# An attention and MLP kernel: eight token tiles in the first group of the second product, and conversions moved behind the split of x

## The chip, the cores and the metric

The program runs on one core of one Trainium2 chip. A core has five engines that follow their own queues in order and meet through semaphores: TensorE (PE; its weight loads are listed apart as PEld), VectorE (DVE), ScalarE (ACT), GpSimd (POOL) and SyncE (SP), which here only starts transfers. The metric is the device time of one execution in microseconds; less is better. Before the change three runs took 959.28, 961.35 and 961.48 us, the median 961.35 us.

## The reference

Attention over 4 batches, 12 heads, 448 positions and head size 64, in which the scores are mixed over the heads before the softmax and after it, and then an MLP over the 1792 x 768 result:

```python
scores = scale * np.matmul(q, k.transpose(0, 1, 3, 2))
scores = np.einsum('bhij,hg->bgij', scores, w_pre)
attn = np.exp(scores - np.max(scores, axis=-1, keepdims=True))
attn = attn / (np.sum(attn, axis=-1, keepdims=True) + 1e-09)
attn = np.einsum('bhij,hg->bgij', attn, w_post)
x = np.matmul(attn, v)          # as (4 * 448, 768)
h = x @ w_in                    # (768, 2048)
g = s * np.maximum(h, 0.0) ** 2 + b
out = g @ w_out                 # (2048, 768)
```

The change lies in the MLP alone. The two weight matrices come as 64-bit floats.

## The kernel before

**Stages.** Attention runs to about 490 us of the trace. The MLP follows in two rounds (`r` 0 and 1), each over half of the 2048 hidden columns: eight tiles `f` of 128. A round has a first product, `gemm1_part` (line 247), which fills a PSUM tile `ph` of 128 hidden columns by the 448 tokens of one batch `b`, and a second product, `gemm2` (line 291), which for each half `oh` of the 768 output columns and each of 14 token tiles `it` of 128 adds up 8 tiles f. Each product is made of three matmuls (high by low, low by high, high by high), so that one token tile of the second product takes 24 matmuls of 384 columns. Round 0 stores its sums to DRAM (`part`), round 1 loads them (`acc`), adds them and writes `out`.

**Weights.** A weight unit is a 128 x 384 piece. Units 0 to 15 of a round are w_in (two for each f), the next 16 are w_out: eight f for oh = 0, then eight for oh = 1. So units 24 to 31 are the weights of oh = 1 in round 0, units 40 to 47 the second half of w_in in round 1, and units 56 to 63 the weights of oh = 1 in round 1. Each is loaded raw (`raw`, two buffers, lines 132 and 139), and then `conversion` (line 145) makes two 32-bit parts of it: one ACT instruction `mk` (line 153) that reads raw, and seven DVE instructions (lines 154 to 177), of which the last writes the low part of `w` (line 177). Only then is the load of the raw after next started on SP (line 180), since a raw buffer comes free. `convert_to(n)` emits conversions up to unit n at that place in the program; on each engine they stand in the order in which they are emitted.

**PSUM.** There are eight banks. Six are handed out in turn by `bank` (line 237), to `ph` tiles and to the tiles of the second product alike. The other two make up one tile with the tag `sc`, which attention used for its scores; the MLP uses it only for the first two `ph` of round 0.

**The second product's groups.** For oh = 0 the first group holds six token tiles (one in each bank of the ring) and goes over f outside and over the six tiles inside, so that a weight of a late f is needed later; then each of the other tiles goes alone over all f. For oh = 1 each tile goes alone from the start, so all eight weights are needed within its first 24 matmuls. When a group is done its tiles are evicted in order: in round 0 by an ACT copy to `ob` (line 307, two buffers) and a store on ACT's queue (line 308); in round 1 by a DVE add into `acc` (line 311), a store on ACT's queue (line 312) and, on SP, the load of the `acc` tile six places further on (line 288), which takes over the buffer of the tile just stored. Six acc tiles are loaded beforehand. After each group the loop emits conversions of the weights of oh = 1:

```python
if oh == 0:
    convert_to(min(u0 + NU + 8 + 2 * (its[-1] - 4), u0 + 2 * NU))
```

With a first group that ends at tile 5 these are two conversions, and two more after each of the next three tiles.

**The start of round 1.** The order of (b, f) is (0, 0) to (0, 3), then (1, 0) to (1, 3), then the rest. The x of batch 1 is kept in the buffers of three g tiles (tile `xg`), which come free when round 0's last matmul is done. So x is split into high and low parts during the first three steps i: two ACT copies each (line 223) and two DVE subtractions (line 232), and after them in each step one conversion (line 913).

Of the kernel before, what the change touches and what calls it, by code (L numbers as in the profile page):

```python
# [9 lines left out]
F32 = mybir.dt.float32  # L10
# [11 lines left out]
def talking_heads_attention__then__act_relu2_kernel(  # L22
# [17 lines left out]
    P = 128  # L40
# [37 lines left out]
    NU = 16  # L78
# [16 lines left out]
    ps = ctx.enter_context(tc.tile_pool(name="ps", bufs=1, space=PSUM))  # L95
# [86 lines left out]
    def convert_step(upto):  # L182

        if done["run"] is None:
            if done["conv"] >= min(upto, len(units)):
                return False
            done["run"] = conversion(done["conv"])
        try:
            next(done["run"])
        except StopIteration:  # L190
            done["run"] = None
            done["conv"] += 1
        return True

    def convert_to(n):
        while convert_step(n):
            pass
# [4 lines left out]
    NT = B * S // P  # L202
# [4 lines left out]
    def load_x(r, b, kc):  # L207
        raw = rp.tile([P, S], F32, tag="xraw", name=f"xraw_{r}_{b}_{kc}", bufs=NKC)
        nc.sync.dma_start(raw, xd[b][kc])
        xraw_t[r, b, kc] = raw  # L210

    def split_x(r, b, kc):
        raw = xraw_t.pop((r, b, kc))
        if b == 1:

            if kc % 2 == 0:
                x_u["g"] = mp.tile(
                    [P, 2, PT], F32R, tag=f"g{kc // 2}_1", name=f"xg_{r}_{kc}", bufs=1
                )
            x = x_u["g"][:, :, kc % 2 * S:kc % 2 * S + S]  # L220
        else:
            x = rp.tile([P, 2, S], F32R, tag="x", name=f"x_{r}_{b}_{kc}", bufs=NKC)
        nc.scalar.activation(x[:, 0, :], raw, AF.Copy)  # L223
        later.append((x[:, 1, :], raw, x[:, 0, :]))
        x_u[r, b, kc] = x
# [3 lines left out]
    def low_parts():  # L229
        while later:  # L230
            o, x, hi = later.pop(0)
            nc.vector.tensor_tensor(out=o, in0=x, in1=hi.bitcast(F32), op=ALU.subtract)  # L232

    banks = ["pm", "po", "pm", "po", "xp", "px"]
    turn = {"bank": 0}

    def bank(name):
        tag = banks[turn["bank"] % len(banks)]
        turn["bank"] += 1
        return ps.tile([P, 512], F32, tag=tag, name=name, bufs=banks.count(tag))  # L240

    def gemm1_part(r, b, f, kc, ph):
        w = w_u["in", r, f, kc // NKH]
        x = x_u[r, b, kc]
        c0 = kc % NKH * P
        for m, (i, y) in enumerate(((0, 1), (1, 0), (0, 0))):
            nc.tensor.matmul(  # L247
                ph[:, :S], w[:, i, c0:c0 + P], x[:, y, :],
                start=(kc == 0 and m == 0), stop=(kc == NKC - 1 and m == 2),
            )  # L250

    def relu2(r, b, f, ph):

        h = mp.tile([P, S], F32, tag="h", name=f"h_{r}_{b}_{f}", bufs=2)
        nc.scalar.activation(h, ph[:, :S], AF.Relu)  # L255
        nc.scalar.activation(h, h, AF.Square)
        nc.scalar.activation(h, h, AF.Identity, scale=sb[:, 0:1], bias=sb[:, 1:2])
        if b % 2 == 0:
            g_t[f, b // 2] = mp.tile(
                [P, 2, PT], F32R, tag=f"g{f}_{b // 2}", name=f"g_{r}_{f}_{b // 2}", bufs=1  # L260
            )
        g = g_t[f, b // 2]
        c0 = b % 2 * S
        nc.scalar.activation(g[:, 0, c0:c0 + S], h, AF.Copy)  # L264
        nc.gpsimd.tensor_tensor(  # L265
            out=g[:, 1, c0:c0 + S], in0=h, in1=g[:, 0, c0:c0 + S].bitcast(F32), op=ALU.subtract
        )
# [18 lines left out]
    def load_acc(oh, it):  # L286
        t = rp.tile([P, S], F32, tag="xraw", name=f"acc_{oh}_{it}", bufs=NKC)[:, :NO]
        nc.sync.dma_start(t, part[oh][it])
        acc_t[oh, it] = t

    def gemm2(r, oh, its):

        pos = [bank(f"po2_{r}_{oh}_{it}") for it in its]
        for f in range(NF):
            w = w_u["out", r, f, oh]
            for po, it in zip(pos, its):
                g = g_t[f, it * P // PT]
                c0 = it % (PT // P) * P
                for m, (x, y) in enumerate(((0, 1), (0, 0), (1, 0))):
                    nc.tensor.matmul(  # L300
                        po[:, :NO], g[:, x, c0:c0 + P], w[:, y, :],
                        start=(f == 0 and m == 0), stop=(f == NF - 1 and m == 2),
                    )
        for po, it in zip(pos, its):
            if r + 1 < NR:
                ob = mp.tile([P, NO], F32, tag="ob", name=f"ob_{oh}_{it}", bufs=2)
                nc.scalar.activation(ob, po[:, :NO], AF.Copy)
                nc.scalar.dma_start(part[oh][it], ob)
                continue
            ob = acc_t.pop((oh, it))  # L310
            nc.vector.tensor_tensor(out=ob, in0=po[:, :NO], in1=ob, op=ALU.add)
            nc.scalar.dma_start(out[it * P:(it + 1) * P, oh * NO:(oh + 1) * NO], ob)
            n = oh * NT + it + NKC
            if n < NOH * NT:
                load_acc(n // NT, n % NT)
# [348 lines left out]
    for ci in range(2, NCH):  # L664
        b, _, _ = chunks[ci]
# [51 lines left out]
    for s in range(NB + 4):  # L717
        spent = max(spent, -0.4) + load.get(s, 0)
        left, held = [], set()
        for x in fill:  # L720
            _, lo, hi, cost, order, f, args = x
# [145 lines left out]
    for r in range(NR):  # L867
        u0 = 2 * r * NU
        n = NHEAD if r == 0 else NF // 2
        order = [(b, f) for b in range(2) for f in range(n)]  # L870
        order += [(b, f) for f in range(n, NF) for b in range(2)]
        order += [(b, f) for b in range(2, B) for f in range(NF)]
        last = {b: i for i, (b, f) in enumerate(order)}
        wait = []

        takes = {0: (r, 2), 2: (r, 3)}
        if r + 1 < NR:
            takes[3] = (r + 1, 0)
        for i, (b, f) in enumerate(order):
            for b0, nxt in takes.items():  # L880
                if i == max(last[b0] - 7, 6):
                    for kc in range(NKC):
                        load_x(*nxt, kc)
            nxt = takes.get(b)
            if r > 0 and i == 0:
                for kc in range(NKC):
                    load_x(r, 1, kc)
            if (r, b) == (0, 0) and f < NHEAD:
                ph = head_t[f]
            else:  # L890
                ph = bank(f"ph_{r}_{b}_{f}")
                for kc in range(NKC):
                    gemm1_part(r, b, f, kc, ph)
                    if nxt and i == last[b] and b < B - 1:
                        split_x(*nxt, kc)
                        low_parts()
            wait.append((r, b, f, ph))

            if not any(i == last[b0] - 1 for b0 in (0, 2)):
                while wait:  # L900
                    relu2(*wait.pop(0))
            if nxt and i == last[b] and b == B - 1:
                for kc in range(NKC):
                    split_x(*nxt, kc)
                    low_parts()
            if r == 0 and b < 2:
                convert_to(min(2 * f + 8, NU))
            if r > 0 and i < 3:
                for kc in (2 * i, 2 * i + 1):
                    split_x(r, 1, kc)  # L910
                    low_parts()
            if r > 0:
                convert_to(u0 + min(i + 9, NU))
            if b == B - 1:
                convert_to(done["conv"] + 1)
        for oh in range(NOH):
            if r + 1 == NR and oh == 0:
                for it in range(NKC):
                    load_acc(0, it)
            if oh == 0:  # L920
                groups = [list(range(6))] + [[it] for it in range(6, NT)]
            else:
                groups = [[it] for it in range(NT)]
            for its in groups:
                gemm2(r, oh, its)
                if oh == 0:
                    convert_to(min(u0 + NU + 8 + 2 * (its[-1] - 4), u0 + 2 * NU))
                elif r + 1 < NR:
                    convert_to(min(u0 + 2 * NU + its[-1] + 1, u0 + 2 * NU + 8))
# [29 lines left out]
```

## Time and profile before

| | us |
|---|---|
| three runs | 959.28, 961.35, 961.48 |
| the profiled execution | 961.09 |
| its span in the trace | 959.4 |
| PE busy | 929.8 (97%) |
| PE weight loads busy | 786.2 (82%) |
| DVE busy | 639.0 (67%) |
| ACT busy | 597.7 (62%) |
| POOL busy | 398.1 (41%) |

The profiled execution took 1.69 us more than its span and lies 0.26 us under the median of the runs, so that a sum made in the trace can be set against the runs as it is. Busy is the union of an engine's instructions; for PE a busy engine is one whose matmuls follow each other, not one at its peak. In the rows a bracket behind an instruction gives the idle time of its engine just before it and what ended it. Shares of busy time say little here, since the MLP has stages with different limits; the rows further down are taken by stage.

### The profile page before, as it was taken

The numbers are of one execution on the slowest core, as the hardware profiler recorded it, in microseconds if no ns is written. First come the engines' busy times: TensorE is split into PE (matmuls) and PEld (weight loads), VectorE is DVE, ScalarE is ACT, GpSimd is POOL, SyncE is SP. The second block draws the span as 40 slices with busy tenths as digits, with TensorE's granted clock in tenths as the row PEclk, the third lists the DMA queues.
The fourth block names the chain that finished last, engine by engine and source line by source line (L and its number), as shares of the span: only waits on it lengthen the run. The fifth ranks groups of instructions, "written<-read, shape, count | busy, mean of one in ns | idle before, by whom it ended". The sixth has DMA issues, their size and how long they took to land.

```text
span 959.4 us, 19910 instructions
## 1 busy us (share of the span) xinstructions
PE 929.8 (97%) x7538; PEld 786.2 (82%) x7538; DVE 639.0 (67%) x1307; ACT 597.7 (62%) x1321; POOL 398.1 (41%) x469
## 2 busy tenths in 40 slices
PE   8899999999999999999999999999999999999998
PEld 4566767777777777777789999999998999999998
DVE  3899999888878888788678217656707711848311
ACT  5678778787888888877777977322216787711000
POOL 3866676666767667766613423100001332310000
PEclk9999999999999999999999999999999999999999
DMA  4665545654455544645323312245431410237431
GB/s 114 173 155 154 151 126 146 180 129 151 106 147 143 135 118 127 157 116 168 112 71 106 109 55 70 66 126 154 132 133 45 154 58 1 82 110 209 145 98 50
DMA packets 124252, 114.63 MB, mean 119 GB/s; under 512 B 61656, under 2 KB 120044, under 8 KB 124156
## 3 DMA queue, kind: packets, MB, share of 16 engines
q1 hardware_dynamic: 114630, 101.69, 38.3%
q10 hardware_dynamic: 9366, 11.59, 3.4%
q8 instruction: 59, 0.97, 0.4%
q14 instruction: 37, 0.30, 0.1%
q0 software_dynamic: 160, 0.09, 0.1%
HBM read 58.28 MB, written 16.52 MB: 78 GB/s over the span
## 4 chain that ended last, share of the span: by engine, by line
PE 64%; ACT 15%; DVE 13%; DMA 5%; issue 2%; POOL 0%; SPq 0%; ACTq 0%; DVEq 0%
PE po L300 24%; PE ph L247 17%; PE xp L517 6%; PE po L621 5%; ACT S L499 5%; PE sc L489 5%; PE pm L578 5%; ACT pm L585 4%; ACT eh L599 3%; DVE eh L606 3%; DVE A L637 2%; DVE st L580 2%; DMA raw<-in_moe_w_out_dram 2%; DMA nq<-in_q_dram 1%; PE trk L442 1%
## 5 line engine op out<-in xcount | busy, mean ns | idle before, releaser
L300 PE MATMUL po<-w,g 128*128 128x384 f32 x1344 | 234.6, 336 | 2.4 <-ACT h L255 2.4
L300 PEld LDWEIGHTS po<-w,g 128*128 128x128 f32 x1344 | 233.7, 188 | 3.1 <-ACT h L255 3.1
L564 POOL TENSOR_TENSOR hl<-blk,hl 120x448 fp32r<-120x448 f32 x180 | 206.0, 1145 | 15.0
L265 POOL TENSOR_TENSOR g<-h,g 128x448 fp32r<-128x448 f32 x64 | 77.9, 1217 | 287.9 <-ACT g L264 274.8
L621 PEld LDWEIGHTS <-eh 120*128 120x128 f16 (+1 forms) x2160 | 115.0, 98 | 63.4 <-DVE eh L606 40.5
L247 PE MATMUL ph<-x,w 128*128 128x448 f32 x810 | 166.2, 364 | 0.0
L247 PEld LDWEIGHTS ph<-x,w 128*128 128x128 f32 x810 | 152.0, 188 | 12.2
L563 POOL TENSOR_SCALAR hl<-blk 120x448 fp32r<-120x448 f32 x180 | 105.1, 584 | 136.2 <-PE pm L578 123.1
L621 PE MATMUL po<-wpost,eh 120*128 120x120 f16 (+1 forms) x2160 | 144.7, 217 | 14.6 <-DVE eh L606 14.1
L585 ACT ACTIVATE pm<-pm,st 120x448 f32<-120x448 f32 x180 | 109.8, 610 | 56.8 <-DVE st L580 56.2
L606 DVE SCALAR_TENSOR_TENSOR eh<-pm,st,eh 120x448 f16<-120x448 f32 x180 | 122.1, 679 | 16.6 <-ACT eh L599 13.2
L599 ACT ACTIVATE eh<-pm,st 120x448 f16<-120x448 f32 x180 | 114.1, 634 | 20.3 <-DVE st L597 17.2
L580 DVE TENSOR_REDUCE st<-pm 120x1 f32<-120x448 f32 x180 | 110.9, 616 | 22.0 <-PE pm L578 20.4
L637 DVE COPY A<-po 128x480 f32<-128x480 f32 x168 | 106.8, 635 | 0.0
L578 PE MATMUL pm<-hl,wpre_hi 120*120 120x448 f32 x360 | 101.9, 364 | 0.7 <-POOL hl L564 0.7
L153 ACT ACTIVATE mk<-raw 128x384 f32<-128x384 f32 x64 | 35.5, 554 | 93.7 <-DMA raw<-in_moe_w_out_dram 43.9
L517 PE MATMUL xp<-A,v 128*64 128x110 f32 (+1 forms) x1536 | 93.7, 265 | 0.0
L499 ACT ACTIVATE S<-sc 110x896 f32<-110x896 f32 (+1 forms) x91 | 83.3, 916 | 13.7 <-PE sc L489 11.5
L489 PE MATMUL sc<-Tk,Tq 64*110 64x448 f32 (+1 forms) x576 | 82.9, 393 | 2.3 <-ACT S L499 1.0
L578 PE MATMUL pm<-hl,wpre_lo 120*120 120x448 f32 x180 | 83.3, 463 | 0.1
L517 PEld LDWEIGHTS xp<-A,v 128*64 128x64 f32 x1536 | 74.2, 136 | 9.9 <-issue 1.2
L232 DVE TENSOR_TENSOR x<-xraw,x 128x448 fp32r<-128x448 f32 x36 | 23.9, 698 | 75.0 <-ACT x L223 75.0
(77 smaller groups left out, 1008.3 us busy)
## 6 DMA issues: line engine op xcount, KB each, us to landing
blk<-S SPq DMA_DIRECT2D x172, 210.0 KB
raw<-in_moe_w_in_dram SPq DMA_DIRECT2D x32, 384.0 KB
raw<-in_moe_w_out_dram SPq DMA_DIRECT2D x32, 384.0 KB
xraw<-xd SPq DMA_DIRECT2D x48, 224.0 KB
part<-ob ACTq DMA_DIRECT2D x28, 192.0 KB
acc<-part SPq DMA_DIRECT2D x28, 192.0 KB
out_dram<-acc ACTq DMA_DIRECT2D x28, 192.0 KB
v<-in_v_dram SPq DMA_DIRECT2D x24, 192.0 KB
```

The lines of the kernel that those rows point to most:

```text
L247: nc.tensor.matmul(ph[:, :S], w[:, i, c0:c0 + P], x[:, y, :], start=(kc == 0 and m == 0), stop=(kc == NKC - 1 and m == 2),)
L300: nc.tensor.matmul(po[:, :NO], g[:, x, c0:c0 + P], w[:, y, :], start=(f == 0 and m == 0), stop=(f == NF - 1 and m == 2),)
L489: nc.tensor.matmul(sc[e][:n, :S], qt[r0:r0 + D, p, x, :n], kt[r0:r0 + D, y, :], start=(m == 0), stop=(m == 2),)
L499: nc.scalar.activation(s_t[ci][:n, 2 * p:2 * p + 2, :], x_t["two"][:n, :, :S], AF.Copy, scale=SCALE)
L517: nc.tensor.matmul(xp[e * D:(e + 1) * D, p % 4, :n], vt[:, e, c, :], a[:, c, 2 * p + e, :n], start=(c == 0), stop=(c == NC - 1),)
L564: nc.gpsimd.tensor_tensor(out=hl[:n, 1, :], in0=blk[:n], in1=hl[:n, 0, :].bitcast(F32), op=ALU.subtract)
L578: nc.tensor.matmul(pm[:n, :S], w[:n, :n], hl[:n, x, :], start=(m == 0), stop=(m == 2))
L580: nc.vector.tensor_reduce(out=st[:n, 0:1], in_=pm[:n, :S], axis=AX.X, op=ALU.max, negate=True)
L585: nc.scalar.activation(e[:n], e[:n], AF.Exp, bias=st[:n, 0:1], accum_out=pm[:n, S:S + 1])
L599: nc.scalar.activation(eh[:n, 0, :], e[:n], AF.Copy, scale=st[:n, 3:4])
L606: nc.vector.scalar_tensor_tensor(out=eh[:n, 1, :], in0=e[:n], scalar=st[:n, 3:4], in1=eh[:n, 0, :], op0=ALU.mult, op1=ALU.subtract,)
L621: nc.tensor.matmul(po[:, c * BP:(c + 1) * BP], eh[:n, x, j0:j0 + P], wpost[:n, y].rearrange("p g i -> p (g i)"), start=(m == 0), stop=(m = ...
```

## The change

The first group of the second product for oh = 0 gets eight token tiles. The two more are put in the two banks of the `sc` tile, and they are the first two of the group; the six of the ring follow. Since the loop's formula is kept, the conversions emitted after that group are six instead of two. At the start of round 1 the conversions of steps 0 to 2 are left out there and come later: one for each step from step 3 on.

```diff
     def gemm2(r, oh, its):
 
-        pos = [bank(f"po2_{r}_{oh}_{it}") for it in its]
+        pos = []
+        if len(its) > len(banks):
+            two = ps.tile([P, 2, 512], F32, tag="sc", name=f"po2_{r}_{oh}")
+            pos = [two[:, 0], two[:, 1]]
+        pos += [bank(f"po2_{r}_{oh}_{it}") for it in its[len(pos):]]
         for f in range(NF):
...
-            if r > 0:
-                convert_to(u0 + min(i + 9, NU))
+            if r > 0 and i > 2:
+                convert_to(u0 + min(i + 6, NU))
...
             if oh == 0:
-                groups = [list(range(6))] + [[it] for it in range(6, NT)]
+                groups = [list(range(8))] + [[it] for it in range(8, NT)]
```

On ACT, behind the first group of round 0 (ob_0_5 is the eviction of tile 5, part its store, mk_24 the first ACT step of conversion 24), there stands before:

```order
L307 ACTIVATE ob_0_5_9577<-po2_0_0_5_9417 128x384
L308 DMA part0_5_71<-ob_0_5_9577 128x384
L153 ACTIVATE mk_24_9581<-raw_24_9354 128x384
L153 ACTIVATE mk_25_9594<-raw_25_9410 128x384
L307 ACTIVATE ob_0_6_9631<-po2_0_0_6_9606 128x384
L308 DMA part0_6_72<-ob_0_6_9631 128x384
L153 ACTIVATE mk_26_9635<-raw_26_9591 128x384
L153 ACTIVATE mk_27_9648<-raw_27_9604 128x384
```

On the same engine at the same place the changed program has (its lines from 294 on are four further down):

```order
L311 ACTIVATE ob_0_5_9626<-po2_0_0_5_9416 128x384
L312 DMA part0_5_71<-ob_0_5_9626 128x384
L311 ACTIVATE ob_0_6_9629<-po2_0_0_6_9417 128x384
L312 DMA part0_6_72<-ob_0_6_9629 128x384
L311 ACTIVATE ob_0_7_9632<-po2_0_0_7_9418 128x384
L312 DMA part0_7_73<-ob_0_7_9632 128x384
L153 ACTIVATE mk_24_9636<-raw_24_9354 128x384
L153 ACTIVATE mk_25_9649<-raw_25_9410 128x384
L153 ACTIVATE mk_26_9662<-raw_26_9646 128x384
L153 ACTIVATE mk_27_9675<-raw_27_9659 128x384
L153 ACTIVATE mk_28_9688<-raw_28_9672 128x384
L153 ACTIVATE mk_29_9701<-raw_29_9685 128x384
```

The evictions of tiles 6 and 7 moved ahead of mk_24, and six mk now stand in a row, with the eviction of tile 8 behind them.

On DVE, behind the first group of round 1 (acc_0_5 is the add of tile 5, u_56 the first DVE step of conversion 56), there stands before:

```order
L311 TENSOR_TENSOR acc_0_4_11523<-po2_1_0_4_11531,acc_0_4_11523 128x384
L311 TENSOR_TENSOR acc_0_5_11525<-po2_1_0_5_11532,acc_0_5_11525 128x384
L154 TENSOR_SCALAR u_56_11703<-raw_56_11475 128x384
L158 SCALAR_TENSOR_TENSOR u_56_11703<-raw_56_11475,u_56_11703 128x384
L162 TENSOR_SCALAR raw_56_11475<-raw_56_11475 128x384
```

On DVE the changed program has there:

```order
L315 TENSOR_TENSOR acc_0_4_11522<-po2_1_0_4_11529,acc_0_4_11522 128x384
L315 TENSOR_TENSOR acc_0_5_11524<-po2_1_0_5_11530,acc_0_5_11524 128x384
L315 TENSOR_TENSOR acc_0_6_11727<-po2_1_0_6_11531,acc_0_6_11727 128x384
L315 TENSOR_TENSOR acc_0_7_11731<-po2_1_0_7_11532,acc_0_7_11731 128x384
L154 TENSOR_SCALAR u_56_11759<-raw_56_11474 128x384
L158 SCALAR_TENSOR_TENSOR u_56_11759<-raw_56_11474,u_56_11759 128x384
```

The adds of tiles 6 and 7, whose acc tiles are not among the six loaded beforehand, moved ahead of conversion 56.

On DVE at the start of round 1 (xg is the split x of batch 1, u_40 the first step of conversion 40) there stands before:

```order
L232 TENSOR_TENSOR xg_1_0_10442<-xraw_1_1_1_10406,xg_1_0_10442 128x448
L154 TENSOR_SCALAR u_40_10449<-raw_40_10193 128x384
L158 SCALAR_TENSOR_TENSOR u_40_10449<-raw_40_10193,u_40_10449 128x384
L162 TENSOR_SCALAR raw_40_10193<-raw_40_10193 128x384
L167 SCALAR_TENSOR_TENSOR w_40_10447<-mk_40_10448,u_40_10449 128x384
L171 SCALAR_TENSOR_TENSOR raw_40_10193<-raw_40_10193 128x384
L175 TENSOR_SCALAR u_40_10449<-w_40_10447 128x384
L177 SCALAR_TENSOR_TENSOR w_40_10447<-raw_40_10193,u_40_10449 128x384
L232 TENSOR_TENSOR xg_1_2_10486<-xraw_1_1_2_10408,xg_1_2_10486 128x448
```

On DVE the changed program has there:

```order
L232 TENSOR_TENSOR xg_1_0_10441<-xraw_1_1_1_10405,xg_1_0_10441 128x448
L232 TENSOR_TENSOR xg_1_2_10472<-xraw_1_1_2_10407,xg_1_2_10472 128x448
L232 TENSOR_TENSOR xg_1_2_10472<-xraw_1_1_3_10409,xg_1_2_10472 128x448
L232 TENSOR_TENSOR xg_1_4_10503<-xraw_1_1_4_10411,xg_1_4_10503 128x448
L232 TENSOR_TENSOR xg_1_4_10503<-xraw_1_1_5_10413,xg_1_4_10503 128x448
L154 TENSOR_SCALAR u_40_10536<-raw_40_10192 128x384
```

All six subtractions stand together, and the conversions moved behind them.

## Rows read from the trace of the kernel before

**Rows 1.** Windows by stage: stretch, length, busy of each engine, granted clock, DMA.
```profile
605.00:718.00 113.00, 113.00 (x652) 113.00 (x651) 58.50 (x131) 26.28 (x53) 1.48 (x1) 1.00 0.40 126
```
**Rows 2.** Waits of PE in the MLP (490 to 960): us, times, longest.
```profile
PE po L300 <- ACT h L255: 2.4, 2, 1.2
PE ph L247 <- DVE xg L232: 1.6, 1, 1.6
```
**Rows 3.** Timeline of PE at its three waits: start us, us, instruction [idle before].
```profile
600.49 2.77 PE L300 MATMUL po<-w,g 128*128 128x384 f32 x15
604.46 7.75 PE L300 MATMUL po<-w,g 128*128 128x384 f32 x43 [1.20 <-ACT h L255]
...
737.44 4.73 PE L247 MATMUL ph<-xg,w 128*128 128x448 f32 x22 [1.55 <-DVE xg L232]
...
841.31 8.96 PE L300 MATMUL po<-w,g 128*128 128x384 f32 x50 [1.24 <-ACT h L255]
```
**Rows 4.** Chain of waits, 570 to 960: start us, us, what.
```profile
600.41 2.93 DMA raw<-in_moe_w_out_dram
...
604.46 114.52 PE po L300 x657
...
828.80 4.97 DMA raw<-in_moe_w_out_dram
...
841.31 114.54 PE po L300 x657
```
**Rows 5.** Timeline of ACT behind the first group of round 0.
```profile
624.55 0.49 ACT L307 ACTIVATE ob<-po 128x384 f32<-128x384 f32 x1 [14.87 <-PE po L300]
...
627.04 0.49 ACT L307 ACTIVATE ob<-po 128x384 f32<-128x384 f32 x1 [1.07 <-DMA part<-ob]
...
631.40 0.56 ACT L153 ACTIVATE mk<-raw 128x384 f32<-128x384 f32 x1 [0.46 <-ACT ob L307]
...
638.85 0.56 ACT L153 ACTIVATE mk<-raw 128x384 f32<-128x384 f32 x1 [5.02 <-DMA raw<-in_moe_w_out_dram]
...
645.54 0.54 ACT L153 ACTIVATE mk<-raw 128x384 f32<-128x384 f32 x1 [3.77 <-DMA raw<-in_moe_w_out_dram]
```
**Rows 6.** Timeline of DVE there: conversions 24, 26 and 31.
```profile
633.59 0.56 DVE L177 SCALAR_TENSOR_TENSOR w<-raw,u 128x384 fp32r<-128x384 uint32 x1
...
641.53 0.56 DVE L177 SCALAR_TENSOR_TENSOR w<-raw,u 128x384 fp32r<-128x384 uint32 x1
...
655.97 0.36 DVE L154 TENSOR_SCALAR u<-raw 128x384 uint32<-128x384 uint32 x1
...
658.63 0.56 DVE L177 SCALAR_TENSOR_TENSOR w<-raw,u 128x384 fp32r<-128x384 uint32 x1
```
**Rows 7.** Timeline of DVE at the start of round 1.
```profile
731.57 1.15 DVE L232 TENSOR_TENSOR xg<-xraw,xg 128x448 fp32r<-128x448 f32 x2
732.63 0.35 DVE L154 TENSOR_SCALAR u<-raw 128x384 uint32<-128x384 uint32 x1
...
736.76 1.15 DVE L232 TENSOR_TENSOR xg<-xraw,xg 128x448 fp32r<-128x448 f32 x2
```
**Rows 8.** Timeline of ACT at the start of round 1: the last copies of xg.
```profile
732.79 1.03 ACT L223 ACTIVATE xg<-xraw 128x448 fp32r<-128x448 f32 x2
```
**Rows 9.** Timeline of DVE behind the first group of round 1.
```profile
861.40 3.16 DVE L311 TENSOR_TENSOR acc<-po,acc 128x384 f32<-128x384 f32 x6 [11.82 <-PE po L300]
864.48 0.35 DVE L154 TENSOR_SCALAR u<-raw 128x384 uint32<-128x384 uint32 x1
...
892.49 0.56 DVE L177 SCALAR_TENSOR_TENSOR w<-raw,u 128x384 fp32r<-128x384 uint32 x1
```
**Rows 10.** Timeline of ACT's queue there: the stores of six tiles.
```profile
861.99 2.95 ACTq L312 DMA_DIRECT2D out_dram<-acc  x6
```
**Rows 11.** Timeline of SP there: the first loads into freed acc buffers.
```profile
863.96 1.94 SPq L288 DMA_DIRECT2D acc<-part  x4
```
**Rows 12.** Windows behind the last matmul, columns as in group 1; granted clock third from last.
```profile
958.50:959.00 0.50, 0.00 (x0) 0.00 (x0) 0.00 (x0) 0.00 (x0) 0.00 (x0) 0.80 0.00 0
```

## The prediction

> **What bounds the kernel now.** First I read the windows by stage, then PE's waits, then PE's timeline at each wait, and last the timelines of the engines it waited for. In the MLP PE does nothing but matmuls: in the long stretch of round 0's second product 113.00 us of 113.00 are busy at a granted clock of 1.00 [rows 1]. Its waits in all of the MLP are three, 4.0 us together [rows 2]: 1.20 us at 604.46 and 1.24 us at 841.31, both in the first group of a second product, and 1.55 us at 737.44, where the first product of batch 1 in round 1 wants the low part of x [rows 3]. The number of matmuls stays, so nothing but these 4.0 us can be won; what can be lost is any slack that the new order uses up.
>
> A matmul of the second product costs 114.52 us / 657 = 0.1743 us, in round 1 the same [rows 4].
>
> **Part 1, the wait at the start of the first group.** Before, 15 matmuls (tiles 0 to 4) run and the 16th waits for the bank of the last ph, which ACT empties late [rows 3]. Now tiles 0 and 1 lie in the scores' banks, which are long empty, so the tile that needs the last ph's bank is tile 7: it is matmul 22, and ACT empties the bank when it did before, at 604.46. Matmul 22 stands where matmul 16 stood: 6 x 0.1743 = 1.05 us are won, 0.15 us of the wait stay. In round 1 the same, 1.05 us.
>
> **Part 2, what the first group holds up in round 0.** Here is the cost. Before, tile 0's last matmul is number 129, and ACT starts its eviction at 624.55 [rows 5]. Now it is number 171; and since the two scores' banks are one tile, the eviction waits for the last matmul of tile 1, number 174. With matmul 22 at 604.46 it starts at 604.46 + 152 x 0.1743 = 630.95; number 129 stood at 604.46 + 113 x 0.1743 = 624.16. So the evictions start 6.80 us later. Two evictions more stand before mk_24, and a pair of them takes 627.04 - 624.55 = 2.49 us, since the third waits for the store of the first [rows 5]. The first mk of the weights for oh = 1 thus moves from 631.40 by 6.8 + 2.45 = 9.25 us to 640.65. DVE waits for it. Conversion 24 ended at 633.59 + 0.56 = 634.15 [rows 6], and now at 643.4.
>
> Seven conversions follow. One takes DVE 658.63 + 0.56 - 655.97 = 3.22 us [rows 6]. Each second one has to wait for its raw load, which starts when the conversion two before it has freed the buffer. These loads landed 638.85 - 634.15 = 4.7 and 645.54 - 642.09 = 3.45 us later [rows 5, 6]; loads elsewhere took 2.93 and 4.97 us [rows 4]. Low bound: 2.93, hidden behind a conversion, weight 31 at 643.4 + 7 x 3.22 = 665.9. High bound: the waits of before, 658.63 + 0.56 + 9.25 = 668.45. I take 3.4, near the second of the two rows in place: 0.2 us more at each of three waits, 666.55. The Trainium skill (DMA: Bandwidth & Descriptors, Issuing engines are not separate DMA queues) says that transfers interleave on the same 16 engines whichever engine issued them. By that the load of 4.7 us was slowed by the store of tile 6 on ACT's queue, which now lies earlier, and 2.93 would hold, 0.65 us less than my sum; by the row of 4.7 it would be 1.9 us more.
>
> When are they needed? Before, oh = 1 began with matmul 337, and weight 31 was needed at matmul 358: 604.46 + 342 x 0.1743 = 664.07, 4.9 us after it was ready at 659.19. That was the cover, and it is used up. Now matmul 358 could start at 604.46 + 336 x 0.1743 = 663.03, and waits until 666.6. Against before round 0 ends 666.6 - 664.07 = 2.6 us later (bounds 1.9 and 4.4), and that holds the 1.05 us of part 1.
>
> The eviction of tile 8 is queued behind mk_29 on ACT. Its bank is wanted by the first tile of oh = 1 at 659.4; mk_29 ends at about 657.5, so it is out in time.
>
> **Part 3, the same in round 1.** Adds start at 861.40 + 6.80 = 868.2 instead of 861.40 [rows 9]. Tiles 6 and 7 need acc tiles whose buffers are still those of tiles 0 and 1: add, store, load, then add. The store of tile 0 is issued 0.59 us after its add began and the load starts 863.96 - 861.99 = 1.97 us later [rows 9 to 11]. The load itself is not seen to land: it is over 0 and under 2.93 us, what a raw load of twice its size took [rows 4]; I take 2.0, like the store of the same 192 KB. Tile 6's add comes at 868.2 + 0.59 + 1.97 + 2.0 = 872.8, tile 7's 0.5 later (loads are issued 1.94 / 4 apart [rows 11]), conversion 56 at 873.8 instead of 864.48 [rows 9]: 9.3 us late. Behind the waiting add all conversions stand, and behind those on SP the raw loads. Weight 63 was ready at 892.49 + 0.56 = 893.05 [rows 9]; two adds (3.16 / 6 = 0.53 us each) no longer stand between, so it is ready at 893.05 + 9.3 - 1.05 = 901.3. It was needed at 841.31 + 342 x 0.1743 = 900.92 and could be at 899.87 now. So round 1 ends 901.35 - 900.92 = 0.45 us later than before. Bounds: acc at hand, eight adds from 868.2 end at 872.4, which makes weight 63 late by nothing and leaves 0.9 us won; a load of 2.93 costs 1.4 us.
>
> **Part 4, the start of round 1.** DVE does conversion 41 from 732.63 on, ahead of the last two subtractions, which start at 736.76 [rows 7], though ACT has their high parts from 732.79 on [rows 8]. Now nothing stands between: they end by about 735, and PE comes to these x at 735.88 [rows 3]. The 1.55 us go, and at the least nothing is lost. The moved conversions (40 to 47, one for each step of 3.6 us) are used from step 8 on and run at steps 3 to 10, unit 40 five steps ahead. On SP three raw loads move behind six x loads, whose buffers are free by then; both are far from their use.
>
> **Sum.** 2.6 - 1.55 + 0.45 = +1.5 us on the profiled execution's 961.09 (span 959.4 and 1.69 around it): 962.6 us. The median of the runs, 961.35, is 0.26 above that execution.
>
> **Rivals.**
> 1. *Slower: raw loads stay slow.* If the loads take what they took in place (4.7 us and so on) and acc's takes 2.93, round 0 loses 4.4 and round 1 loses 1.4: 4.4 - 1.55 + 1.4 = +4.25, 965.3 us. It decides from about 3.9 us for a load on. For it: 4.7 and 4.97 us are in the rows [rows 4 to 6]. Against it: the evictions that store beside them now lie earlier. Chance 0.18.
> 2. *The clock falls.* Round 0's wait now comes in pieces, about 0.9 us before weight 30 and 2.7 us before weight 31. Waits of up to 1.55 us left the granted clock at 1.00 (2.4 GHz) [rows 1, 3]; behind the last matmul, which ended at 955.85 [rows 4], it fell about 3 us later: the mean of 958.50 to 959.00 is 0.80 [rows 12]. If it falls here, matmuls take up to 2 x 0.1743; over half of a tile's 24 that is 2.1 us: 964.7 us. [...] No wait of that length between matmuls is in this trace. Chance 0.12.
> 3. *Part 4 gains nothing,* since the subtractions meet POOL or a late copy: 1.55 us more, 964.1 us. Against it: the rows show DVE on a conversion, not on a slow subtraction [rows 7]. Chance 0.08.
> 4. *Faster: the weights of oh = 1 are not late.* Then the three gains stand alone, 1.05 + 1.55 + 1.05 = 3.65: 957.4 us. Weight 31 would have to be there at 663.0, seven conversions in 19.6 us, 2.8 each; DVE alone needs 3.22 [rows 6]. Chance 0.07.
>
> **How the numbers follow.** My forecast has 0.55, and its own range is 961.2 to 964.2. To hold 8 in 10 the range goes to 960.3 below, where both rounds lie at their low bounds (1.9 - 1.55 - 0.9 = -0.55), and to 966.0 above, over rival 1. About 0.3%, 2.9 us, is what can be told from no change here. Slower by more: most of rival 1, over half of rival 2, half of rival 3 and a tenth of my forecast, 0.29. Faster: 0.06, nearly all rival 4. The rest, 0.65, is the same.
>
> **What would show it.** PE's timeline after: a wait of about 0.2 us instead of 1.2 in each first group; none before the second group of xg; new waits for the line that writes w's low part, some 3.5 us in all about 21 matmuls into oh = 1 of round 0, and about 1.4 us there in round 1. ACT's first mk of those weights comes some 9 us later, and DVE's sixth add in round 1 is followed by a wait for acc. If no such new wait is there, part 2 is wrong; if they are longer and the granted clock stays 1.00, the loads are.

## The result, and the profile after

The changed kernel is slower: 970.25 us in the median (967.81 to 972.54, four runs) against 960.4 us before, ratio 1.0102 with a 95% interval of 1.0072 to 1.0132. I had forecast 962.6 us, with 966.0 as the upper end. The profiled execution took 969.51 us, its span is 967.8 us, 8.4 us more than before.

PE's waits in the MLP after the change (us, times, longest), which answer to [rows 2]:

```profile
PE po L304 <- DVE w L177: 6.6, 3, 2.5
PE po L304 <- DVE acc L315: 0.9, 1, 0.9
PE po L304 <- ACT h L255: 0.2, 1, 0.2
```

The three old waits are gone but for 0.2 us. In their place stand waits for weights (line 177 writes the low part of w) and one for an add that empties a bank. They were 4.0 us together and are 7.8 us now, added up from the timeline. PE's timeline shows where they lie, to be held against [rows 3]:

```profile
604.55 7.73 PE L304 MATMUL po<-w,g 128*128 128x384 f32 x43 [0.25 <-ACT h L255]
...
664.81 1.08 PE L304 MATMUL po<-w,g 128*128 128x384 f32 x3 [2.02 <-DVE w L177]
668.06 22.22 PE L304 MATMUL po<-w,g 128*128 128x384 f32 x116 [2.17 <-DVE w L177]
...
739.25 14.76 PE L247 MATMUL ph<-xg,w 128*128 128x448 f32 x72
...
901.18 4.02 PE L304 MATMUL po<-w,g 128*128 128x384 f32 x21 [0.94 <-DVE acc L315]
907.66 17.56 PE L304 MATMUL po<-w,g 128*128 128x384 f32 x91 [2.46 <-DVE w L177]
```

All 72 matmuls on xg now follow each other: the wait of 1.55 us is won. In each round the first token tile of oh = 1 waits for its last weights. But 116 matmuls took 22.22 us behind the second wait, where 0.1743 each makes 20.2. The windows there say why (columns as in group 1, the granted clock third from last):

```profile
661.00:665.00 4.00, 1.98 (x12) 1.67 (x11) 3.75 (x9) 0.88 (x2) 0.00 (x0) 1.00 0.44 137
665.00:665.25 0.25, 0.25 (x2) 0.25 (x2) 0.21 (x2) 0.25 (x2) 0.00 (x0) 0.73 0.00 0
665.00:668.00 3.00, 0.89 (x3) 0.38 (x2) 2.82 (x7) 1.11 (x3) 0.00 (x0) 0.52 0.63 209
668.00:672.00 4.00, 3.94 (x12) 3.94 (x13) 0.92 (x3) 1.11 (x3) 0.00 (x0) 0.51 0.72 238
...
907.50:911.00 3.50, 3.34 (x11) 3.34 (x12) 2.90 (x7) 0.00 (x0) 0.00 (x0) 0.52 0.48 168
```

The granted clock fell to half, 1.2 GHz instead of 2.4. In round 0 it fell at about 665.1, while the three matmuls behind the first wait ran (0.73 is the mean of 665.00 to 665.25), stayed there through the second wait and was back at about 671.9. In round 1 it fell at about 907.5, at the end of the wait of 2.46 us, and was back at about 910.9. PE is busy nearly all through 668 to 672 and does 12 matmuls there, where 23 would fit.

The chain of work that ended last has, behind the first group of round 1, a store, a load and a raw load where [rows 4] had nothing but matmuls:

```profile
874.17 2.08 DMA out_dram<-acc
876.31 3.63 DMA acc<-part
...
884.42 3.17 DMA raw<-in_moe_w_out_dram
```

The load of 3.63 us on it is the fourth acc load, that of tile 9; the two for which adds wait are told further down.

Cut by PE's timelines into three stretches, the MLP compares as follows (A: round 0's first L300 or L304 matmul to round 1's first of L247; B: from there to round 1's second product; C: that to the end of the last matmul; us, the experiments' profiles below):

| kernel | A | B | C |
|---|---|---|---|
| before | 118.33 | 118.48 | 118.55 |
| changed | 124.30 | 116.60 | 122.88 |
| e1: x split alone | 118.40 | 116.60 | 117.94 |
| e2: eight tiles alone | 124.81 | 118.25 | 123.01 |
| e3: four ahead | 117.72 | 116.60 | 117.87 |
| e4: dummies | 123.29 | 116.59 | 122.55 |
| e5: four ahead, round 0 | 117.46 | 116.59 | 122.38 |
| e6: four ahead, round 1 | 123.83 | 116.60 | 117.4 |
| e7: six tiles, four ahead | 118.48 | 116.60 | 119.73 |
| e8: between | 124.12 | 116.59 | 119.15 |
| e10: four ahead, two later | 117.01 | 116.60 | 116.98 |
| e11: six tiles, four ahead, two later | 117.71 | 116.60 | 118.10 |

672 matmuls of 0.1743 us make 117.1, and e10 with 117.0 shows that A and C have no more than that to win. The change costs 6.0 us in A and 4.3 in C and wins 1.9 in B, 8.4 together. There is one profile of each kernel, and A begins between 598.9 and 600.7 us in them, so that spans also differ by up to 1.8 us through what lies ahead of A; the stretches are the better measure.

### The profile page after: what moved, and what is told of

Read it like the earlier page. It is cut to its first block, busy times and chain, and to the rows that moved or that the text cites. A ratio compares the mean times of both kernels' runs of the same rounds, so it can differ in the third digit from the quotient of the medians.

```text
span 967.8 us, 19903 instructions
## 1 busy us (share of the span) xinstructions
PE 934.1 (97%) x7538; PEld 789.6 (82%) x7538; DVE 640.0 (66%) x1307; ACT 598.3 (62%) x1321; POOL 399.5 (41%) x469
## 4 chain that ended last, share of the span: by engine, by line
PE 59%; DVE 17%; ACT 16%; DMA 5%; issue 2%; POOL 0%; ACTq 0%; SPq 0%; DVEq 0%
PE ph L247 18%; PE po L304 18%; PE xp L521 6%; PE po L625 5%; ACT S L503 5%; PE sc L493 5%; PE pm L582 4%; ACT pm L589 4%; ACT eh L603 3%; DVE eh L610 3%; DVE A L641 2%; DVE st L584 2%; DMA raw<-in_moe_w_out_dram 2%; DVE w L167 2%; DVE w L177 1%
## 5 line engine op out<-in xcount | busy, mean ns | idle before, releaser
L304 PE MATMUL po<-w,g 128*128 128x384 f32 x1344 | 239.4, 340 | 7.9 <-DVE w L177 6.6
L304 PEld LDWEIGHTS po<-w,g 128*128 128x128 f32 x1344 | 236.6, 190 | 10.5 <-DVE w L177 7.8
L247 PE MATMUL ph<-x,w 128*128 128x448 f32 x810 | 166.1, 365 | 0.0
L247 PEld LDWEIGHTS ph<-x,w 128*128 128x128 f32 x810 | 152.1, 188 | 12.0
L582 PEld LDWEIGHTS pm<-hl,wpre_hi 120*120 120x120 f32 x360 | 65.5, 182 | 5.6 <-POOL hl L568 1.0
```

Of the source, the lines that this page charges most:

```text
L247: nc.tensor.matmul(ph[:, :S], w[:, i, c0:c0 + P], x[:, y, :], start=(kc == 0 and m == 0), stop=(kc == NKC - 1 and m == 2),)
L304: nc.tensor.matmul(po[:, :NO], g[:, x, c0:c0 + P], w[:, y, :], start=(f == 0 and m == 0), stop=(f == NF - 1 and m == 2),)
L582: nc.tensor.matmul(pm[:n, :S], w[:n, :n], hl[:n, x, :], start=(m == 0), stop=(m == 2))
```

## The experiments

My theory after the result: late weights and the half clock behind them are all of the loss. The rivals: the eight banks, or the moved conversions, are slow by themselves.

**e1, the second edit alone**, on the kernel before:

```diff
-            if r > 0:
-                convert_to(u0 + min(i + 9, NU))
+            if r > 0 and i > 2:
+                convert_to(u0 + min(i + 6, NU))
```

> Of the change only its last edit: the conversions of round 1 behind the split of x; the first group keeps six tiles. If the edits act apart, the wait of 1.55 us before the second group of xg goes and the two waits of 1.2 us stay: span 1.55 us under the kernel before, ratio 0.998. If the moved conversions are part of the loss (the rival: they come late for the later steps of round 1), the span is above that of before.

Measured: 958.52 us against 959.42, ratio 0.9991 (0.9980 to 1.0002). By the time alone there might be no gain; in the profile B is 1.9 us shorter and the wait is gone. The moved conversions cost nothing.

**e2, the eight tiles alone**: the edit of e1 taken back in the changed kernel.

```diff
-            if r > 0 and i > 2:
-                convert_to(u0 + min(i + 6, NU))
+            if r > 0:
+                convert_to(u0 + min(i + 9, NU))
```

> Of the change only the group of eight; the conversions of round 1 stand where they stood before. If all the loss lies in late weights of oh = 1 and the half clock behind them, the span is that of the changed kernel and 1.55 us more (about 969.4), with the wait before xg back. If the moved conversions carry the loss, it falls to 958 or less, since two waits of 1.05 us are won.

Measured: 971.5 us, ratio 1.0127 (1.0112 to 1.0142), span 969.0. B is back at 118.25, A and C are as bad as in the changed kernel. All of the loss is in the group of eight.

**e3, four conversions ahead of the group**, on the changed kernel:

```diff
             for its in groups:
+                if oh == 0 and len(its) > 1:
+                    convert_to(u0 + NU + 8 + 4)
                 gemm2(r, oh, its)
```

> The changed kernel, but four of the eight conversions for oh = 1 are emitted ahead of the group of eight, so that on ACT and DVE they stand ahead of its evictions, in the time in which both engines were idle. If the evictions ahead of the conversions are the cause, no weight of oh = 1 is late, the granted clock stays at 1.00 in both stretches, and the three gains stand alone: 1.05 + 1.55 + 1.05 = 3.65 us under before, span about 955.7, ratio 0.996. If the eight banks themselves cost (the rival: matmuls into the scores' banks are slower, or the evictions of eight), a loss stays without any wait for weights.

Measured: 957.16 us, ratio 0.9978 (0.9969 to 0.9987), span 955.3. PE's only waits in the MLP are these:

```profile
PE po L304 <- ACT h L255: 1.0, 2, 0.6
```

The eight tiles are kept and 12.5 us of span come back, 11.6 of them in A and C, so neither the scores' banks nor the evictions of eight are slow in themselves: the place of the conversions decides.

**e4, dummies in the waits**, on the changed kernel:

```diff
+        fill = ({6: 11, 7: 12}, {0: 5, 7: 14})[r] if oh == 1 and its == [0] else {}
+        if fill:
+            idle = ps.tile([P, 2, 512], F32, tag="sc", name=f"idle_{r}")
         for f in range(NF):
+            for _ in range(fill.get(f, 0)):
+                nc.tensor.matmul(
+                    idle[:, 0, :NO], g_t[0, 0][:, 0, :P], w_u["out", r, 0, 1][:, 0, :],
+                    start=True, stop=True,
+                )
```

> The changed kernel, and in the waits of oh = 1's first token tile PE runs matmuls whose result nobody reads, in the scores' bank, 23 in round 0 (ahead of f = 6 and f = 7) and 19 in round 1 (ahead of f = 0 and f = 7). The weights are as late as before. If the half clock behind the waits is a cost of its own, it stays at 1.00 and some 4.3 us come back: span about 963.5 of 967.8. If the loss is the late weights alone, and the clock only goes along with it, nothing comes back: 967 to 968.

Measured: 966.97 us, ratio 1.0080 (1.0067 to 1.0094), span 964.9. PE in round 0 (idle is the tile of the dummies):

```profile
661.66 2.07 PE L303 MATMUL idle<-w,g 128*128 128x384 f32 x11
663.97 0.79 PE L312 MATMUL po<-w,g 128*128 128x384 f32 x3 [0.23 <-DVE w L177]
664.60 2.24 PE L303 MATMUL idle<-w,g 128*128 128x384 f32 x12
667.22 12.99 PE L312 MATMUL po<-w,g 128*128 128x384 f32 x73 [0.38 <-DVE w L177]
```

and its window at the place where the clock had been at half:

```profile
668.00:672.00 4.00, 4.00 (x25) 4.00 (x24) 0.27 (x1) 1.36 (x4) 0.00 (x0) 1.00 0.59 199
```

The weights are even later than in the changed kernel (667.22 is 68.3 us from round 0's first L312 matmul, against 67.6; in round 1 it is 67.4 against 66.3), the clock stays at 1.00, and 25 matmuls stand in the 4 us. From weight f = 7 on, round 0 takes 722.20 - 667.22 = 55.0 us instead of 724.79 - 668.06 = 56.7, and round 1 55.1 instead of 56.6: the half clock costs 1.75 and 1.5 us, 3.2 together. That is less than the 4.3 expected. And since the last weights came 0.7 and 1.1 us later, only 1.3 us of it are left in A and C; the other 1.6 us of the shorter span lie ahead of A. In the time the intervals of this kernel and the changed one overlap, so the split by weights and clock rests on the profiles. The mean granted clock of each execution, which is on record, bears it out: 0.994 to 0.995 in all four of the changed kernel, 1.000 in all six with dummies.

**e5 and e6, four ahead in round 0 only and in round 1 only**, on the changed kernel:

```diff
+                if oh == 0 and len(its) > 1 and r == 0:      # e6: r == 1
+                    convert_to(u0 + NU + 8 + 4)
```

> The changed kernel with four conversions emitted ahead of the group of eight in round 0 only. If each round pays its own late weights and its own half clock, round 0's second product (124.3 us from its first matmul to round 1's first) falls to about 117.5, round 1's stays at 122.9, and the span is near 961. If round 1 is late only because round 0 was (the rival), both fall and the span is near 956.

> The same in round 1 only. If the rounds pay apart, round 0 stays at 124.3 us, round 1's second product falls from 122.9 us to about 117.5, and the span is near 962.5. If round 1's loss hangs on round 0's, it falls less and the span stays near 967.

Measured: 962.56 us, ratio 1.0029 (1.0017 to 1.0042), and 963.03 us, ratio 1.0035 (1.0023 to 1.0047). A heals in e5 alone and C in e6 alone: each round pays for itself. In e5 round 1 still waits

```profile
895.40 4.03 PE L304 MATMUL po<-w,g 128*128 128x384 f32 x21 [1.61 <-DVE acc L315]
901.89 55.13 PE L304 MATMUL po<-w,g 128*128 128x384 f32 x315 [2.46 <-DVE w L177]
```

and its 315 matmuls take 55.13 us: here the same 2.46 us of waiting left the clock at full speed. The profiled execution is the exception in this: its mean granted clock is 0.999, that of the seven others 0.996 to 0.998. So what a wait of this length does to the clock differs between executions.

**e8, the old order behind the group of eight**: two conversions each behind the evictions of tiles 5, 6 and 7.

```diff
+    def between(r, oh, its, it):
+        if oh == 0 and len(its) > 1 and it > 4:
+            convert_to(2 * r * NU + NU + 8 + 2 * (it - 4))
...
+                between(r, oh, its, it)
...
+            between(r, oh, its, it)
```

> The changed kernel, with the old order behind the group of eight: two conversions behind tile 5's eviction, two behind tile 6's, two behind tile 7's. If what I sized too small are the two evictions ahead of the conversions (in round 0 their stores, in round 1 the waits for acc tiles), the first mk comes 2.5 us sooner in round 0 and conversion 56 some 4.4 us sooner in round 1; a wait of about 2 us stays in round 0 and under 1 us in round 1, the granted clock stays at 1.00 in at least one of them, and the span is 960 to 962. If the eight tiles' length alone makes the weights late (the rival), two waits of 2 us each stay in round 0, 2 us in round 1, and the span is 965 or more.

Measured: 964.49 us (960.58 to 966.74), ratio 1.0042 (1.0027 to 1.0058): between the two. The waits:

```profile
662.90 0.79 PE L308 MATMUL po<-w,g 128*128 128x384 f32 x3 [1.24 <-DVE w L177]
666.16 14.07 PE L308 MATMUL po<-w,g 128*128 128x384 f32 x66 [2.46 <-DVE w L177]
...
904.05 55.14 PE L308 MATMUL po<-w,g 128*128 128x384 f32 x315 [0.94 <-DVE w L177]
```

In round 1 the expectation holds: without the waits for acc tiles 3.4 us of waiting become 0.94. In round 0 it fails: 3.7 us stay of 4.2, though two evictions no longer stand ahead, and the clock falls again. The first mk comes 1.65 us sooner there instead of 2.5 (40.04 us from the first matmul, 41.69 in the changed kernel), since the eviction of tile 4 waits 3.29 us for a store; and DVE waits 1.3 us between the conversions, 0.94 of it for a raw load, against 0.3 in the changed kernel. The rest of the lateness is the longer group. The mean granted clock of the seven executions lies between 1.000 (the fastest, 960.58 us) and 0.995 (the slowest, 966.74): with one and the same program it fell in some executions and hardly or not in others.

**e10, e3 with two conversions later**, so that no mk waits for its raw load ahead of ACT's emptying of the last ph:

```diff
-            if b == B - 1:
+            if b == B - 1 and f < NF - 2:
                 convert_to(done["conv"] + 1)
```

> The kernel with four conversions ahead of the group of eight in both rounds, and the two conversions of the last two steps of a round's first product moved behind that product too, so that no mk that waits for its raw load stands ahead of the emptying of the last ph on ACT. If the rest of PE's waits (0.39 and 0.61 us at the start of the group) hang on that mk, they go: 1.0 us less than with four ahead alone, span about 954.3, ratio to before about 0.997. If ACT is late for another reason, the waits stay and the ratio is that of four ahead, 0.998.

Measured: 955.25 us against 960.38, ratio 0.9955 (0.9942 to 0.9967), the fastest kernel here. PE waits for nothing in the MLP, and A and C are 1.6 us shorter than in e3, where 1.0 was expected:

```profile
599.60:716.60 117.00, 117.00 (x674) 116.74 (x673) 62.56 (x139) 29.82 (x58) 2.55 (x2) 1.00 0.39 125
833.20:950.00 116.80, 116.80 (x673) 116.65 (x671) 50.44 (x105) 10.29 (x19) 3.84 (x3) 1.00 0.40 127
```

**e7 and e11, six tiles instead of eight in e3 and e10**, so the kernel before with the edit of e1, that of e3, and in e11 that of e10 too:

```diff
-                groups = [list(range(8))] + [[it] for it in range(8, NT)]
+                groups = [list(range(6))] + [[it] for it in range(6, NT)]
```

> The kernel before with the split of x ahead of round 1's conversions and four conversions ahead of the first group, which keeps six tiles. If the eight tiles win what my sum gave them (1.05 us a round), the two waits of 1.2 us stay here and the span is some 1.4 us above the like kernel with eight tiles (waits of 0.39 and 0.61 us there): ratio near 0.999. If the eight tiles win nothing by themselves, the ratio is the 0.998 of that kernel.

> The same with six tiles, and the last two conversions of each first product moved behind it. If the wait at the start of the group hangs on the mk ahead of ACT's emptying of the last ph, it goes with six tiles as well, PE has no wait in the MLP, and the ratio is the 0.9955 of the like kernel with eight tiles: the eight tiles then buy nothing. If six tiles leave too little time for the emptying even so, a wait stays and the ratio is 0.997 or more.

Measured: 960.2 us, ratio 1.0003 (0.9994 to 1.0013), and 957.62 us, ratio 0.9983 (0.9974 to 0.9992); with eight tiles 0.9978 and 0.9955. In e7 the two waits for ph stay as expected (1.35 and 1.18 us). I was wrong on e11: the wait for ph goes, but two new ones come behind the shorter group, for banks whose eviction is late:

```profile
625.89 14.33 PE L300 MATMUL po<-w,g 128*128 128x384 f32 x81 [0.62 <-ACT ob L307]
...
860.43 92.12 PE L300 MATMUL po<-w,g 128*128 128x384 f32 x528 [0.87 <-DVE acc L311]
```

So the eight tiles are worth some 0.25% once conversions go ahead of them: in A and C 2.6 us between e7 and e3, 1.8 between e11 and e10.

## Why the prediction was wrong

The mechanism was the one forecast: the weights of oh = 1 come later and PE waits for them in its first token tile. Three terms of the sum were too small: the two evictions ahead of mk_24 in round 0, the acc loads in round 1, and the clock, which the sum put at nothing.

**Part 1 and part 4 held.** Matmul 22 waited 0.25 us instead of 1.20, and the wait before xg is gone (e1: 0.64 to 1.28 us stay in the groups of six, none before xg).

**Part 2, round 0: "a pair of them takes 627.04 - 624.55 = 2.49 us".** This is the step that failed in round 0; the seven conversions behind it took 23.1 us, raw loads included, as I had worked out. ACT behind the first group, to be held against [rows 5]:

```profile
631.38 0.49 ACT L311 ACTIVATE ob<-po 128x384 f32<-128x384 f32 x1 [21.61 <-PE po L304]
...
633.86 0.49 ACT L311 ACTIVATE ob<-po 128x384 f32<-128x384 f32 x1 [1.06 <-DMA part<-ob]
634.38 0.33 ACTq L312 DMA_DIRECT2D part<-ob  x1
...
637.90 0.49 ACT L311 ACTIVATE ob<-po 128x384 f32<-128x384 f32 x1 [2.60 <-DMA part<-ob]
...
642.18 0.55 ACT L153 ACTIVATE mk<-raw 128x384 f32<-128x384 f32 x1 [0.40 <-ACT ob L311]
```

The evictions start at 631.38, as worked out (624.55 + 6.80). But the eviction of tile 4 waits 2.60 us for the store of tile 2, issued at 634.38; the pair of tiles 2 and 3 takes 637.90 - 633.86 = 4.04 us, and the first mk comes at 642.18 instead of 640.65. Weight 31 is ready at 668.01 instead of 666.55, 1.5 us later, all of it from that store. The forecast loss of 2.6 us against before became 4.0.

**Part 3, round 1: "I take 2.0, like the store".** DVE, to be held against [rows 9]:

```profile
872.15 2.88 DVE L315 TENSOR_TENSOR acc<-po,acc 128x384 f32<-128x384 f32 x6 [18.39 <-PE po L304]
877.80 0.56 DVE L315 TENSOR_TENSOR acc<-po,acc 128x384 f32<-128x384 f32 x1 [2.77 <-DMA acc<-part]
878.99 0.56 DVE L315 TENSOR_TENSOR acc<-po,acc 128x384 f32<-128x384 f32 x1 [0.64 <-DMA acc<-part]
879.47 0.35 DVE L154 TENSOR_SCALAR u<-raw 128x384 uint32<-128x384 uint32 x1
...
887.69 0.36 DVE L154 TENSOR_SCALAR u<-raw 128x384 uint32<-128x384 uint32 x1 [1.72 <-DMA raw<-in_moe_w_out_dram]
...
900.58 0.55 DVE L315 TENSOR_TENSOR acc<-po,acc 128x384 f32<-128x384 f32 x1
...
907.05 0.56 DVE L177 SCALAR_TENSOR_TENSOR w<-raw,u 128x384 fp32r<-128x384 uint32 x1
```

The wait is where I put it, but the acc loads took longer. SP issues that of tile 6 at 874.72 and that of tile 7 at 875.26, beside the stores of ACT's queue:

```profile
874.72 0.32 SPq L288 DMA_DIRECT2D acc<-part  x1
875.26 0.32 SPq L288 DMA_DIRECT2D acc<-part  x1
...
872.74 7.18 ACTq L316 DMA_DIRECT2D out_dram<-acc  x8
```

The first is issued when I had it, 2.6 us behind the first add. But the adds of tiles 6 and 7 start 3.1 and 3.7 us behind the issue of their loads, where I had taken 2.0. The bound of 2.93, which I drew from a transfer of twice the size, did not hold for the second. The Trainium skill (DMA: Bandwidth & Descriptors, Issuing engines are not separate DMA queues) says that transfers run on the same engines and interleave there, whichever engine started them; the trace fits that, since these loads ran beside the eight stores. That the stores slowed them was not tried. Behind the adds, the raw load of conversion 58 stood on SP behind acc loads that wait for stores:

```profile
881.88 2.45 SPq L288 DMA_DIRECT2D acc<-part  x2
884.42 1.90 SPq L139 DMA_DIRECT2D raw<-in_moe_w_out_dram  x2
```

Counted from round 1's first L304 matmul (841.39), conversion 56 begins at 38.1 us instead of 36.5 (873.8 - 837.30), and weight 63 is ready at 66.2 instead of 64.0. The add of tile 8 (900.58), behind six conversions, held up the first tile's bank by 0.94 us, which my sum did not price in round 1; it lost nothing more, since weight 63 came later still. e8 takes the waiting adds out of this chain, and 2.5 us of round 1's waits go.

**The rival that I held for 0.12, the clock, is what I sized worst.** I saw the 3 us behind the last matmul and took shorter waits for safe. But in round 0 the clock fell 0.3 us behind the end of a wait of 2.02 us, and in round 1 at the end of one of 2.46 us. I also priced it for one round at 2.1 us, and it came in both, at 3.2 (e4). The Trainium skill (TensorE: Matmul & The Clock Gate, HAM oscillation) tells of a kernel that waits for a transfer between its groups of matmuls and starts each next group at the low clock. Its waits are longer than these; here the clock fell all the same, to 0.52 in the mean of 907.5 to 911. e5 shows that it isn't certain.

So of the some 6.9 us between my sum (+1.5) and the profile (+8.4), 1.5 is the store in round 0, 2.2 the acc loads and SP in round 1, and 3.2 the clock. B won 0.3 us more than forecast, and as much is left over in A and C.

**Rival 4**, that the weights aren't late, was no story about this kernel, but it named the better one: ahead of the first evictions ACT had been idle for 14.87 us in round 0 [rows 5] and DVE for 11.82 in round 1 [rows 9]. e3 puts four conversions there, and A, B and C together are 3.2 us shorter than before, where the three gains make 3.65. (Its span is 4.1 us shorter; the 0.9 between lie ahead of A.)

## What to carry to other kernels

When a group is made longer, look at what is emitted behind it: the work for the next stage starts later by the length of the group and by its evictions, and has less time left until it is needed. Before the group is lengthened, move that work ahead of it, into the time in which its engines wait for the group to end. A wait that is late by conversions recurs with each of them (3.26 us apart here, 0.52 us of matmuls between), and such a series of waits may cost the clock as well as itself, so price both. And bound a store or a load by the slowest like it in the trace, not by the nearest row.

## What was not expected of the hardware

- A wait of 2.46 us between matmuls left the clock at half behind it in the changed kernel's round 1 and at full speed in e5's, at the same place of the program. With matmuls in the waits it stayed at 1.00 (e4). And the fall need not come within the wait: in e2's round 1 the wait of 2.47 us ended at 908.76, and the clock fell at about 909.7, with PE busy since:

```profile
909.50:910.00 0.50, 0.50 (x4) 0.50 (x3) 0.50 (x2) 0.00 (x0) 0.00 (x0) 0.74 0.14 33
```

- The store of tile 2 in round 0 took 3.5 us (issued at 634.38, waited for until 637.90); before, a store issued at the end of the first eviction was waited for until 627.04, about 2 us [rows 5]. And in e2, e4, e8 and e10 the same eviction waited 3.3 to 3.5 us. In its stretch, 634.3 to 637.9, the queues show one transfer beside the stores, an instruction load, which in the kernel before came outside of the evictions (624.5 to 631):

```profile
q10 hardware_dynamic: 291, 0.39, 30.4%
q8 instruction: 1, 0.02, 2.1%
```

In e6, whose round 0 is the changed kernel's, this load came some 0.8 us later, and the store of tile 3, not that of tile 2, was the slow one (issued at 635.49, waited for until 638.73). That the instruction load slows the store was not tried and stays open. A store as slow stands in the trace of before as well, beside raw loads: issued at 656.60, waited for until 660.21.
